# A new written-out order for a fused attention and expert kernel: SBUF work of two engines kept apart, four shared banks, seven fp32 dummies

## The chip, the cores and the metric

The kernel runs on one core of a Trainium2 chip. A core has five engines that run side by side and wait for each other through semaphores: TensorE (PE in the profile; its weight loads are PEld), VectorE (DVE), ScalarE (ACT), GpSimd (POOL) and SyncE (SP), which here only issues DMA transfers. Products of TensorE go to PSUM, eight banks of 128 x 512 fp32; everything else lives in SBUF. The metric is the device time of one execution in microseconds, the median of several.

## The reference

Inputs are `r`, `k`, `v`, `w` of shape 4 x 8 x 768 x 48 (batch, heads, time, head width), `u` of 8 x 48, and two weight matrices, 384 x 2048 and 2048 x 384. First a recurrent attention:

```python
for t in range(S):
    cur = einsum('bhd,bhe->bhde', u * k[t], v[t])
    y[t] = einsum('bhd,bhde->bhe', r[t], state + cur)
    state = w[t][..., None] * state + einsum('bhd,bhe->bhde', k[t], v[t])
```

Its output, as 3072 tokens of 384, goes through `h = x @ w_in`, `g = max(h, 0) ** 2`, and `out = g @ w_out`.

## The kernel before

**Tiling.** Time is cut into steps of 256 positions, three for each of the four batches: steps 0 to 11. Inside a step the recurrence is done by chunks of 128 in matrix form. Decays are multiplied up as sums of logarithms: `ww_` multiplies neighbouring w, `lw_` takes the logarithm, `cum_` sums it by a product with a triangle of ones into a PSUM tile `att`, `al_` forms a second exponent from the first, and `exp_` exponentiates. `rw_`, `kw_`, `ku_`, `qp_`, `vq_` are elementwise multiplies of SBUF tiles; `q_` is a sum over a row and `qs_`, `vs_`, `v_` are copies that cast or move rows. `rd_` multiplies r or k by the decays. The results are transposed, by TensorE (`tr_`, then the copy `rkt_`) in steps 0 to 3, and by DMA (`dtr_`) from step 4 on. Then `p_` multiplies keys by queries, `pm_` applies the mask, `su_`, `ts_` and `sn_` carry the state on, `y_` and `yc_` form the output, `ysb_` adds the term of the own position, and the result is transposed to `xT`, by TensorE (`yt_`, then `xt_`) in steps 0 to 5 and by DMA (`dyt_`) from step 6 on.

**The expert part.** For each step there are eight `m1_` (six products of 128 x 256 into one bank: two blocks of `x @ w_in`), eight `rl_` that evict such a bank with max(x, 0) into fp16, four `sq_` that square two of these groups, eight `m2_` (four products of 128 x 384, two output halves by four quarters of the sum), and two `os_` that evict the finished sum, each followed by a `store`. The weights come in eight fp32 blocks (`ld.n.i`, `ld.n.o`) and are cast to bf16 (`cast`). Block n of W_in serves `m1_` groups 2n and 2n + 1.

**PSUM.** Two `att` tiles take four banks. The other four are two named `bk` (numbers 0 and 1) and two named `m1_bank` (2 and 3). Before the change `m1_` (line 532) can use only the second pair and `m2_` (line 559) and its `os_` (line 566) only the first; transposes can go to any (`bf16_bank`), and a `p_` or a `su_` goes to an `att` tile, or split over a pair, where the letter `b` or `m` says so. A split `p_` is masked by two instructions (line 431) rather than one (line 434).

**Order.** `ORDER` (line 17) is a list of 864 words. Each names an operation, its step and part, the bank after a colon, and the engine after `=` where there is a choice (A ScalarE, V VectorE, G GpSimd). The operations are issued in this order, so each engine's own list, SP's list of loads, transposes and stores included, is the order of its words here; nothing reorders it on the chip. Where two engines depend on each other semaphores make them wait. `warm_.n.b` issues n dummy products of a cleared tile into bank b (4 and 5 are the `att` tiles); their results are never read.

What the prediction speaks of most is the part of `ORDER` up to the first `m1_`, the list of VectorE in it, and the spacing of `dtr_` to `p_`, `dyt_` to `m1_`, and `m1_` to `rl_`.

Of the kernel before, what the change touches and what calls it, by code (L numbers as in the profile page):

```python
# [22 lines left out]
tr_.1.0:1 ww_.2=G ld.2.i v_.1=A rkt_.1.0=V ysb_.0=V vs_.1.1=A warm_.4.2 p_.1.1:0 qp_.1=G su_.1:m ld.2.v
pm_.1.1 lw_.2 yt_.0:0 cum_.2:1 ld.3.i ts_.1.0=V rw_.2=G q_.1 exp_.2 kw_.2=G xt_.0=V vs_.1.0=A rd_.2.0 qs_.1=G
ac_.2 cast.i.1=A rd_.2.1 warm_.10.1 tr_.2.0:1 sn_.1.0 p_.1.0:0 ku_.2=G ts_.1.1=V yc_.1.1:1 tr_.2.1:0
cast.i.0=A pm_.1.0 ld.0.o m1_.0.3:0 ld.3.w rkt_.2.1=V m1_.0.2:1 vq_.1=G rkt_.2.0=V y_.1:1 rl_.0.3=A yc_.1.0:1
rl_.0.2=V p_.2.0:0 m1_.0.1:0 ld.1.o ysb_.1=V cast.i.2=G m1_.0.0:1 rl_.0.1=A pm_.2.0 yt_.1:0 ld.3.r rl_.0.0=A
m1_.0.5:0 v_.2=A xt_.1=V qp_.2=G sn_.1.1 m1_.0.4:1 rl_.0.5=A p_.2.1:1 su_.2:b sq_.0.0=A rl_.0.4=V ld.2.o
m1_.1.4:0 cast.i.3=G ts_.2.0=V pm_.2.1 m1_.1.5:1 rl_.1.4=A q_.2 sn_.2.0 m1_.1.3:0 rl_.1.5=A ld.3.o vs_.2.1=G
vs_.2.0=A yc_.2.0:0 yc_.2.1:0 rl_.1.3=V m1_.1.6:1 cast.o.0=G qs_.2=A m1_.1.0:0 ld.3.k rl_.1.6=V sq_.0.2=A  # L30
y_.2:0 rl_.1.0=V m1_.1.1:1 vq_.2=G m1_.1.7:0 rl_.1.1=V ld.3.v m2_.0.1.0:0 sq_.1.2=A rl_.1.7=V sq_.0.1=A
cast.o.1=G m1_.1.2:1 rl_.1.2=A ysb_.2=V m1_.0.7:0 ld.4.w ww_.3=G yt_.2:1 rl_.0.7=V m1_.0.6:1 xt_.2=V m2_.0.1.1
sq_.1.1=A rl_.0.6=V ld.5.w m1_.2.6:0 cast.o.2=G lw_.3 sq_.1.0=A rl_.2.6=A cum_.3:1 sq_.1.3=A rw_.3=G al_.3
ld.5.r m2_.0.0.0:1 m1_.2.7:1 m2_.0.0.1 cast.o.3=V exp_.3 sq_.0.3=A ld.4.k rd_.3.0 kw_.3=G m1_.2.1:0 rl_.2.7=A
ac_.3 m2_.0.1.2 m2_.0.0.2 rl_.2.1=V ku_.3=G m2_.0.0.3 rd_.3.1 ld.4.v m2_.0.1.3 vs_.3.0=A m1_.2.0:1 os_.0.1=V
qp_.3=G ld.5.v m1_.2.3:0 os_.0.0=V rl_.2.0=V tr_.3.1:0 rl_.2.3=A tr_.3.0:1 rkt_.3.1=V v_.3=A ld.4.r m1_.2.4:1
ww_.4=G rkt_.3.0=V m2_.1.0.0:0 rl_.2.4=A q_.3 ww_.5=G p_.3.1:0 vs_.3.1=A ld.6.k su_.3:1 pm_.3.1 p_.3.0:m
m2_.1.0.1 ts_.3.0=A lw_.4 sn_.3.0 ld.5.k pm_.3.0 m2_.1.0.2 qs_.3=A m2_.1.1.0:1 sq_.2.0=A vq_.3=G ts_.3.1=V
m2_.1.0.3 ld.6.w cum_.4:0 m2_.1.1.1 ku_.4=G ac_.4 al_.4 store.0.1 m1_.2.5:0 os_.1.0=A v_.5=A yc_.3.1:1 y_.3:1
lw_.5 kw_.4=G m1_.2.2:1 ld.6.r ysb_.3=V rl_.2.5=A m2_.1.1.2 exp_.4 sn_.3.1 rl_.2.2=V yt_.3:0 rw_.4=G cum_.5:1  # L40
xt_.3=V m2_.1.1.3 vs_.4.0=A ac_.5 sq_.2.1=A qp_.4=G al_.5 m1_.3.0:0 rd_.4.1 v_.4=A m1_.3.3:1 rd_.4.0 dtr_.4.1
m2_.2.0.0:0 rl_.3.0=A rw_.5=G rl_.3.3=A m2_.2.0.1 os_.1.1=V exp_.5 q_.4 dtr_.4.0 su_.4:0 sq_.2.2=A m1_.3.4:0
kw_.5=G rd_.5.0 ww_.6=G m2_.2.1.0:1 rl_.3.4=A ts_.4.0=V sq_.2.3=A m1_.3.5:1 vs_.4.1=A rd_.5.1 sn_.4.0
m2_.2.1.1 store.1.0 ts_.4.1=V rl_.3.5=V ku_.5=G m1_.3.6:0 store.1.1 m2_.2.1.2 qs_.4=A ld.7.w ld.6.v rw_.6=G
p_.4.1:1 rl_.3.6=A p_.4.0:0 pm_.4.1 pm_.4.0 m2_.2.1.3 lw_.6 vq_.4=G m1_.3.1:1 m1_.3.2:0 rl_.3.1=A su_.5:1
dtr_.5.1 dtr_.5.0 vs_.5.1=G sq_.3.0=A rl_.3.2=V yc_.4.0:0 yc_.4.1:0 sn_.4.1 y_.4:0 os_.2.1=V sq_.3.1=A
m1_.3.7:1 ysb_.4=V ld.7.v m2_.2.0.2 rl_.3.7=A ld.8.w kw_.6=G vs_.5.0=G yt_.4:1 ld.7.k sq_.3.3=A m2_.2.0.3
xt_.4=V cum_.6:0 al_.6 m1_.4.4:0 qp_.5=G os_.2.0=A ac_.6 m1_.4.7:1 ts_.5.0=V exp_.6 rl_.4.4=V m2_.3.0.0:1
rl_.4.7=A rd_.6.1 m1_.4.6:0 rd_.6.0 m2_.3.0.1 dtr_.6.1 m2_.3.1.0:0 ku_.6=G qp_.6=G sq_.3.2=A rl_.4.6=A q_.5
dtr_.6.0 p_.5.0:1 p_.5.1:0 vs_.6.0=A m1_.4.5:1 sn_.5.0 m2_.3.0.2 qs_.5=G rl_.4.5=A pm_.5.1 pm_.5.0 vq_.5=G  # L50
m1_.4.1:0 m1_.4.3:1 rl_.4.3=A store.2.1 ld.8.v m2_.3.0.3 rl_.4.1=V ld.8.k v_.6=A ww_.7=G y_.5:0 q_.6 os_.3.0=A
ld.7.r m1_.4.0:1 store.0.0 ld.9.k ww_.8=G yc_.5.0:0 qs_.6=A su_.6:1 yc_.5.1:0 ysb_.5=V vs_.6.1=A ts_.6.0=V
m1_.4.2:0 ld.8.r m2_.3.1.1 rl_.4.0=V yt_.5:1 xt_.5=V sn_.6.0 lw_.7 vq_.6=G rl_.4.2=A p_.6.0:0 m2_.3.1.2
sq_.4.3=A store.2.0 pm_.6.0 m1_.5.2:1 ku_.7=G m1_.5.6:0 ts_.6.1=V yc_.6.1:0 sq_.4.0=A rl_.5.2=A p_.6.1:1
rl_.5.6=A m2_.3.1.3 kw_.7=G pm_.6.1 sq_.4.2=A m1_.5.4:1 rw_.7=G m1_.5.3:0 os_.3.1=V rl_.5.4=A y_.6:0 sn_.6.1
rl_.5.3=A cum_.7:1 kw_.8=G ysb_.6=V al_.7 m2_.4.0.0:1 vs_.7.1=A m1_.5.7:1 m1_.5.5:0 v_.7=G dyt_.6 sq_.4.1=A
rl_.5.7=V qp_.7=G rl_.5.5=V m2_.4.1.0:0 exp_.7 ld.9.w ld.9.v m2_.4.0.1 ac_.7 rd_.7.0 sq_.5.1=A m2_.4.0.2
ku_.8=G rd_.7.1 sq_.5.3=A dtr_.7.0 m2_.4.0.3 m1_.5.0:1 lw_.8 m1_.5.1:0 rw_.8=G rl_.5.0=V su_.7:0 q_.7
rl_.5.1=A cum_.8:1 dtr_.7.1 m1_.6.3:1 qs_.7=A m1_.6.5:0 rl_.6.3=V ld.10.w qp_.8=G ac_.8 sq_.5.0=A m2_.4.1.1
os_.4.0=V ts_.7.0=V ld.11.w sn_.7.0 m1_.6.4:1 rl_.6.5=A al_.8 ww_.9=G m2_.4.1.2 ld.9.r rl_.6.4=V exp_.8  # L60
store.3.0 m2_.5.1.0:1 sq_.5.2=A rd_.8.1 ts_.7.1=V sn_.7.1 m1_.6.0:0 vs_.7.0=G vs_.9.1=A rd_.8.0 m2_.4.1.3
m2_.5.1.1 kw_.9=G rl_.6.0=A dtr_.8.0 p_.7.1:0 v_.8=A p_.7.0:1 vq_.7=G pm_.7.1 m1_.6.1:1 m2_.5.1.2 rl_.6.1=A
pm_.7.0 ku_.9=G m2_.5.1.3 sq_.6.0=A lw_.9 m1_.6.6:0 dtr_.8.1 store.3.1 q_.8 yc_.7.0:0 v_.9=A yc_.7.1:0
rl_.6.6=V rw_.9=G su_.8:1 y_.7:0 os_.5.1=A ts_.8.0=V m1_.6.2:1 ysb_.7=V os_.4.1=A cum_.9:1 m1_.6.7:0 al_.9
dyt_.7 m2_.5.0.0:1 rl_.6.2=V exp_.9 ww_.10=G rl_.6.7=V m2_.5.0.1 ac_.9 ld.10.r rd_.9.1 sq_.6.1=A sq_.6.2=A
sn_.8.0 qp_.9=G ld.10.k qs_.8=G store.4.1 m2_.5.0.2 ld.10.v rd_.9.0 m2_.5.0.3 m2_.6.1.0:0 vs_.8.1=G sq_.6.3=A
dtr_.9.0 vs_.8.0=A p_.8.0:m p_.8.1:0 pm_.8.0 su_.9:1 m2_.6.1.1 ts_.9.0=A pm_.8.1 m2_.6.1.2 lw_.10 m1_.7.4:0
# [564 lines left out]
```

## Time and profile before

| what | value |
|---|---|
| median of the runs | 182.77 us (lowest 182.61) |
| profiled execution, first to last instruction | 182.2 us |
| TensorE busy | 171.8 us |
| VectorE, ScalarE, GpSimd busy | 130.0, 132.7, 122.7 us |
| bytes moved by DMA | 35.8 MB |
| first `m1_` product | 26.99 us |
| end of the last `m2_` product | 178.84 us |

One of the three runs took 960.62 us; the median leaves it aside. The profiled execution's own time is its span, 182.2 us, and what lies outside the first and the last instruction; the median of the runs is 0.57 us longer than that span. Times in the profile count from the first instruction. A row of groups gives line, engine, operation, output and inputs, shapes and count, then busy microseconds, mean nanoseconds of one, and the idle time ahead of them with what ended it. A row of the timeline gives start and duration. In a row of the chain of waits stand start, duration, engine or queue, tile and line.

### The profile page before, as it was taken

Reading aid. Unit: us, or ns where it says so; the run is one execution under the profiler, and the core shown is the slowest. Engines: PE = TensorE matmul, PEld = TensorE weight load, DVE = VectorE, ACT = ScalarE, POOL = GpSimd, SP = SyncE. Lnnn points to the kernel's source line nnn. Section 1 sums busy time; section 2 is a strip of 40 time slices with the busy share of each in tenths; the row PEclk is TensorE's granted clock in tenths of the full one; section 3 lists DMA queues with packets and bytes.
Section 4 is the critical chain, followed back from the end, with each engine's and each line's share of the span. In section 5 each row is a group of like instructions: output and inputs, shape, how many; then the busy total and the mean of one; then the engine's idle time right before and its main releaser. Section 6 shows DMA issues by size and latency. Waiting matters only on the chain.

```text
span 182.2 us, 5695 instructions
## 1 busy us (share of the span) xinstructions
PE 171.8 (94%) x2385; PEld 123.4 (68%) x2385; DVE 130.0 (71%) x195; ACT 132.7 (73%) x235; POOL 122.7 (67%) x140
## 2 busy tenths in 40 slices
...
GB/s 138 263 263 240 221 359 350 337 314 311 234 274 230 261 158 270 99 247 130 239 296 205 193 270 172 252 189 193 171 109 195 150 47 0 86 144 33 0 86 130
DMA packets 79208, 35.81 MB, mean 197 GB/s; under 512 B 72400, under 2 KB 77648, under 8 KB 79184
## 3 DMA queue, kind: packets, MB, share of 16 engines
...
## 4 chain that ended last, share of the span: by engine, by line
PE 75%; SPq 10%; DMA 8%; ACT 4%; issue 1%; DVE 1%; ACTq 0%
PE bk L561 32%; PE m L536 32%; SPq L178 8%; DMA w_st<-in_moe_w_in_dram 5%; PE att L420 3%; DMA rT<-rdec_buf 2%; PE att L483 2%; PE att L493 2%; PE att L446 1%; ACT gt L545 1%; PE att L326 1%; ACT wi_sb L200 1%; PE bk L516 1%; SPq L188 1%; SPq L205 1%
## 5 line engine op out<-in xcount | busy, mean ns | idle before, releaser
L536 PE MATMUL m<-xT,wi_sb 128*128 128x256 bf16 x576 | 74.0, 273 | 1.3 <-ACT gt L545 1.2
L561 PE MATMUL bk<-wo_sb,gt 128*128 128x384 bf16 x384 | 71.9, 326 | 0.0
L536 PEld LDWEIGHTS <-wi_sb 128*128 128x128 bf16 x576 | 54.8, 98 | 13.0 <-issue 0.9
L561 PEld LDWEIGHTS <-gt 128*128 128x128 bf16 x384 | 36.9, 98 | 19.2
L545 ACT ACTIVATE gt<-m 128x512 f16<-128x512 f32 x56 | 33.0, 595 | 22.3 <-PE m L536 21.9
L553 ACT ACTIVATE gt<-gt 128x1024 bf16<-128x1024 f16 x42 | 43.3, 1051 | 1.4 <-DVE gt L547 1.1
L547 DVE TENSOR_SCALAR gt<-m 128x512 f16<-128x512 f32 x40 | 27.0, 686 | 9.6 <-PE m L536 9.3
L434 DVE TENSOR_TENSOR pmT<-att,mask 128x1024 bf16<-128x1024 f32 x20 | 23.9, 1218 | 4.5 <-PE att L420 4.5
L297 POOL TENSOR_TENSOR ku<-k_raw,u_bc 128x768 f32<-128x768 f32 x12 | 21.8, 1819 | 0.2 <-DMA u_bc<-in_u_dram 0.2
L302 POOL TENSOR_TENSOR ku<-ku,r_raw 128x768 f32<-128x768 f32 x11 | 20.7, 1881 | 0.2
L316 POOL TENSOR_TENSOR ku<-v_sh,qs 128x768 f32<-128x768 bf16 x11 | 16.3, 1479 | 4.9 <-ACT qs L277 4.8
L277 ACT CAST v_sh<-v_raw 64x384 bf16<-64x384 f32 x34 | 17.3, 508 | 0.4
L290 POOL TENSOR_TENSOR k_raw<-k_raw,w_raw 128x384 f32<-128x384 f32 x12 | 12.2, 1013 | 6.4 <-DMA k_raw<-in_k_dram 6.3
L286 POOL TENSOR_TENSOR r_raw<-r_raw,w_raw 128x384 f32<-128x384 f32 x12 | 12.0, 1000 | 6.4 <-DMA r_raw<-in_r_dram 6.4
L504 DVE TENSOR_TENSOR y_sb<-att,ku 128x768 bf16<-128x768 f32 x12 | 11.4, 953 | 5.5 <-issue 1.6
L461 POOL TENSOR_TENSOR S<-t_state,ac_buf 128x192 bf16<-128x192 f32 x20 | 10.2, 512 | 6.4 <-DVE t_state L456 3.4
L361 DVE TENSOR_TENSOR kdec_buf<-k_raw,att 128x768 bf16<-128x768 f32 x12 | 11.4, 949 | 3.4 <-ACT att L340 2.8
L358 DVE TENSOR_TENSOR rdec_buf<-r_raw,att 128x384 bf16<-128x384 f32 x24 | 12.1, 547 | 2.2 <-ACT att L340 1.1
L340 ACT ACTIVATE att<-att 128x768 f32<-128x768 f32 x12 | 9.6, 798 | 3.1 <-PE att L328 1.9
L568 ACT ACTIVATE o_sb<-bk 128x384 f32<-128x384 f32 x13 | 6.3, 485 | 7.4 <-PE bk L561 7.3
L307 DVE TENSOR_REDUCE q<-ku 128x16 f32<-128x768 f32 x12 | 11.3, 943 | 0.0
L578 PE MATMUL att<-warm 128*128 128x512 bf16 x27 | 9.1, 492 | 1.2 <-DVE half_ones L228 1.2
...
## 6 DMA issues: line engine op xcount, KB each, us to landing
...
rT<-rdec_buf SPq DMA_TRANSPOSE x16, 4.1
```

Of the source, the lines that this page charges most:

```text
L178: nc.sync.dma_start(out=t[:, hs, at:at + 2, :].rearrange("p h j d -> p h (j d)"), in_=src[b, hs, i * T:(i + 1) * T, :].rearrange("h (p j) ...
L277: copy(out[j * Q:(j + 1) * Q, c], src[c * Q:(c + 1) * Q, :, j])
L290: tensor_mul("kw_", s, h)(raw["k", s][:, hs, 0, :], raw["k", s][:, hs, 1, :], raw["w", s][:, hs, 1, :])
L297: tensor_mul("ku_", s, h)(tiles["ku", s][:, hs], raw["k", s][:, hs, 1:3, :], u_bc[:, hs, None, :].to_broadcast([C, n, 2, D]))
L302: tensor_mul("qp_", s, h)(ku, ku, raw["r", s][:, heads(h), 0:2, :])
L316: tensor_mul("vq_", s)(vq[:], tiles["vs", s][:], tiles["qs", s][:, :, :, None].to_broadcast([C, 2, H, D]))
L434: nc.vector.tensor_mul(pmT, ps_p[:].rearrange("p e (x t) -> p (e x) t", t=C), mk.to_broadcast([C, 8, C]))
L536: nc.tensor.matmul(ps1[:, j, :], wi_sb[:, n // 4, kk, n % 4 * 128:(n % 4 + 1) * 128], tiles["xT", s][:, :, kk, :], start=(kk == 0), stop=( ...
L545: nc.scalar.activation(rl, m1, AF.Relu, scale=RS)
L547: nc.vector.tensor_scalar(out=rl, in0=m1, scalar1=RS, scalar2=0.0, op0=ALU.mult, op1=ALU.max)
L553: nc.scalar.activation(gt, rl, AF.Square)
L561: nc.tensor.matmul(m2, gt[:, n, c * C:(c + 1) * C], wo_sb[:, n, :], start=(n == 0), stop=(n == NT - 1))
```

## The change

The whole of `ORDER` is replaced: same operations for the same steps, in another sequence, with other engines and other banks. Counted by words: on VectorE `ku_` 0 to 1, `kw_` 0 to 3, `rw_` 0 to 3, `qp_` 1 to 4, `vq_` 1 to 3, `ww_` 2 to 4, `vs_` 0 to 2, `sq_` 6 to 8, `cast` 1 to 2, `rl_` 40 to 35, `xt_` 6 to 3, with the reverse on GpSimd or ScalarE. Split `p_` go from four to seven. The words `warm_` go from eight, with 46 bf16 products, to three with seven products of fp32. Besides, `m1_`, `m2_` and `os_` take a bank number from 0 to 3, and an `m2_` sum begins with whichever quarter comes first in the list rather than with quarter 0.

```diff
 ORDER = """
-ld.0.w ld.0.k ld.0.r ld.0.u ld.1.w ww_.0=V lw_.0 warm_.11.5 cum_.0:0 kw_.0=G exp_.0 rd_.0.1 ld.0.v warm_.8.5
...
+ld.0.w ww_.0=V lw_.0 ld.0.r rw_.0=G warm_.3.4 cum_.0:0 exp_.0 rd_.0.0 ld.0.k kw_.0=G rd_.0.1 ld.1.w ww_.1=G
+ac_.0 lw_.1 warm_.2.5 tr_.0.0:0 tr_.0.1:2 cum_.1:0 rkt_.0.1=A ld.0.u rkt_.0.0=V ku_.0=V qp_.0=V ac_.1 q_.0
+exp_.1 p_.0.0:m ld.1.k ld.0.v ld.1.r p_.0.1:b pm_.0.1 qs_.0=A v_.0=A vs_.0.1=A kw_.1=G rd_.1.1 vs_.0.0=A
+rw_.1=V ku_.1=G qp_.1=G rd_.1.0 warm_.2.5 tr_.1.1:1 rkt_.1.1=A su_.0:1 ts_.0.0=V sn_.0.0 tr_.1.0:0 vq_.0=G
+rkt_.1.0=A pm_.0.0 y_.0:0 ts_.0.1=V ld.1.v v_.1=A sn_.0.1 ld.2.w yc_.0.1 p_.1.1:1 q_.1 pm_.1.1 vs_.1.1=A
+p_.1.0:b su_.1:m ww_.2=G ts_.1.0=V qs_.1=A ysb_.0=V pm_.1.0 yc_.1.0:1 ld.2.r sn_.1.0 ld.2.k yc_.1.1 lw_.2
+vs_.1.0=A ts_.1.1=V cum_.2:0 yt_.0:0 y_.1 kw_.2=V rw_.2=G exp_.2 rd_.2.0 rd_.2.1 vq_.1=G xt_.0=A tr_.2.0:1
+ld.1.i sn_.1.1 ld.0.i ac_.2 rkt_.2.0=A tr_.2.1:3 ysb_.1=V cast.i.1=G yt_.1:0 rkt_.2.1=V cast.i.0=A ld.2.i
+ku_.2=G yc_.2.0:1 p_.2.0:m xt_.1=V ld.2.v qp_.2=G p_.2.1:0 cast.i.2=G m1_.1.3:1 m1_.0.2:0 pm_.2.0 m1_.0.3:3
...
 """
@@
+    quad = bk + m1_bank
@@
-    warm = consts.tile([C, 512], BF16)
+    warm = consts.tile([C, 512], FP32)
@@ def m1_(s, g):
-        ps1 = tiles["m1", s, g] = m1_bank[int(slot["m1_", s, g])][:].rearrange("p (j t) -> p j t", j=2)
+        ps1 = tiles["m1", s, g] = quad[int(slot["m1_", s, g])][:].rearrange("p (j t) -> p j t", j=2)
@@
+    summed = {}
+
     def m2_(s, c, q):
         gt = tiles["gt", s]
-        m2 = bk[int(slot["m2_", s, c])][:, 0:DM]
-        for n in range(4 * q, 4 * q + 4):
-            nc.tensor.matmul(m2, gt[:, n, c * C:(c + 1) * C], wo_sb[:, n, :],
-                             start=(n == 0), stop=(n == NT - 1))
+        m2 = quad[int(slot["m2_", s, c])][:, 0:DM]
+        summed[s, c] = summed.get((s, c), 0) + 1
+        for n in range(4):
+            nc.tensor.matmul(m2, gt[:, 4 * q + n, c * C:(c + 1) * C], wo_sb[:, 4 * q + n, :],
+                             start=(summed[s, c] == 1 and n == 0), stop=(summed[s, c] == NT // 4 and n == 3))
@@ def os_(s, c):
-        m2 = bk[int(slot["m2_", s, c])]
+        m2 = quad[int(slot["m2_", s, c])]
@@ def warm_(n, i):
-            nc.tensor.matmul((bk + m1_bank)[i][:] if i < 4 else att[i - 4][:, 0, :], warm[:, 0:C], warm[:],
+            nc.tensor.matmul(quad[i][:] if i < 4 else att[i - 4][:, 0, :], warm[:, 0:C], warm[:],
                              start=True, stop=True)
```

The words around the transposes of step 9 read in the new list:

```
m1_.7.3:2 rl_.7.3=A sq_.6.2=A rw_.9=G lw_.10 ysb_.8=V m1_.7.2:3 rl_.7.2=V m1_.7.6:1 ld.9.v m1_.6.7:2 rl_.7.6=V
...
m1_.8.4:1 al_.10 ld.10.k os_.5.1=A m1_.8.3:3 m1_.8.2:2 vs_.9.1=G m1_.8.7:0 rl_.8.4=V dtr_.9.1 m1_.8.5:1 q_.9
dtr_.9.0 rl_.8.7=V sn_.9.0 sq_.7.2=A rl_.8.2=A rl_.8.3=A ac_.10 sq_.6.0=A m1_.7.1:2 m1_.8.1:0 m1_.8.0:3
ts_.9.1=V rl_.8.5=V rl_.7.1=A sq_.6.3=V ld.11.w rl_.8.1=A sq_.7.3=A m1_.8.6:2 vs_.9.0=A rl_.8.0=V p_.9.1:b
```

138 lines of the change are left out of this document (63 added, 75 removed).

## Prediction

> **What bounds the kernel now.** I read the page first, then the table of stretches, then the chain of waits, the timeline around the start, and the groups by form.
>
> ```profile
> PE 171.8 (94%) x2385; PEld 123.4 (68%) x2385; DVE 130.0 (71%) x195; ACT 132.7 (73%) x235; POOL 122.7 (67%) x140
> ```
>
> TensorE is busy 94% of the span; no other engine reaches 75%. The table of stretches (us, then busy PE, PEld, DVE, ACT, POOL with counts, granted clock, DMA share, GB/s) says where the missing 6% lies:
>
> ```profile
> 0.00:10.00 10.00, 8.81 (x39) 3.64 (x40) 4.78 (x12) 4.19 (x8) 6.01 (x17) 1.00 0.91 207
> 10.00:20.00 10.00, 7.40 (x141) 4.24 (x138) 8.89 (x12) 8.43 (x19) 7.25 (x8) 1.00 1.15 245
> 20.00:27.00 7.00, 5.63 (x119) 3.53 (x119) 6.64 (x11) 4.86 (x8) 6.61 (x10) 1.00 0.96 304
> 27.00:30.00 3.00, 2.34 (x63) 2.00 (x60) 3.00 (x5) 1.45 (x2) 1.27 (x1) 1.00 1.07 338
> 30.00:40.00 10.00, 9.40 (x153) 8.10 (x154) 7.40 (x11) 8.65 (x17) 9.16 (x9) 1.00 1.08 333
> ...
> 80.00:90.00 10.00, 9.45 (x190) 7.29 (x187) 7.24 (x10) 7.73 (x16) 8.77 (x13) 1.00 1.03 193
> ...
> 120.00:130.00 10.00, 9.92 (x109) 7.45 (x108) 7.01 (x10) 8.82 (x20) 9.73 (x10) 1.00 0.85 160
> ...
> 170.00:179.00 9.00, 8.83 (x59) 5.48 (x56) 1.56 (x3) 3.56 (x6) 0.00 (x0) 1.00 0.24 87
> ```
>
> From 27 us on TensorE is without work for only 0.66 + 0.60 + 0.55 + 0.08 + 0.17 = 2.1 us; every stretch left out here shows 10.00. So the run has three parts: a start of 27 us, a body of products without holes, a tail. The next rows, from the timeline (start, duration) and the chain, date them: the first dummies, the first exp, ten later dummies, the first W_in product (`m1_`), the cast of the W_in block that came last, and the end of the last products.
>
> ```profile
> 1.19 4.87 PE L578 MATMUL att<-warm 128*128 128x512 bf16 x11 [1.19 <-DVE half_ones L228]
> 6.84 0.80 ACT L340 ACTIVATE att<-att 128x768 f32<-128x768 f32 x1 [1.10 <-PE att L328]
> 22.11 2.32 PE L578 MATMUL bk<-warm 128*128 128x512 bf16 x10
> 26.99 1.47 PE L536 MATMUL m<-xT,wi_sb 128*128 128x256 bf16 x12
> 28.55 1.47 ACT L200 CAST wi_sb<-w_st 128x1536 bf16<-128x1536 f32 x1 [1.84 <-DMA w_st<-in_moe_w_in_dram]
> ...
> 171.68 7.16 PE bk L561 x44
> ```
>
> The body runs from 26.99 to 178.84: **151.85 us**. What follows (last eviction, store, landing) is 182.2 - 178.84 = **3.36 us**. The median of the runs, 182.77, stands 0.57 above this execution's span, which I add at the end.
>
> **The change, part by part.** The products themselves stay: 96 `m1_`, 96 `m2_`, and every product of the attention part occurs as often as before. An order cannot shorten a body without holes; it can only start it earlier, put more work ahead of it, or close holes. So the sum is: start of the body + 151.85 - work done ahead + change in holes + tail.
>
> *Work done ahead.* Ahead of the first `m1_` the new TensorE list has everything that the old one has there, and besides `y_.1`, `yc_.1.0`, `yc_.2.0`, `yt_.1`, `p_.2.0` and `p_.2.1`. The chain prices such pieces: two `yc_` (x32), a whole `y_`, a `yt_`, two `p_` (x32).
>
> ```profile
> 36.54 0.37 PE att L493 x32
> ...
> 72.03 0.51 PE att L483 x16
> ...
> 73.84 0.34 PE bk L516 x6
> ...
> 79.01 0.58 PE att L420 x32
> ```
>
> That is 0.37 + 0.51 + 0.34 + 0.58 = **1.80 us** off the body.
>
> *Start of the body.* The loads ahead of W_in blocks 1 and 0 are the same twelve inputs and `u`, in another order, so the blocks should land when they landed (cast of block 0 possible at 28.55, block 1 before that). Block 1, used first, is now cast by GpSimd, after `vq_.1` and `sn_.1.1`. But the first `m1_` of the new list is for step 1, and VectorE must by then have done both steps' share, `ysb_.1` and `xt_.1` last. Its list up to there, priced by groups (mean ns after the comma):
>
> ```profile
> L434 DVE TENSOR_TENSOR pmT<-att,mask 128x1024 bf16<-128x1024 f32 x20 | 23.9, 1218 | 4.5 <-PE att L420 4.5
> ...
> L358 DVE TENSOR_TENSOR rdec_buf<-r_raw,att 128x384 bf16<-128x384 f32 x24 | 12.1, 547 | 2.2 <-ACT att L340 1.1 <-ACT ac_buf L346 1.1
> ...
> L504 DVE TENSOR_TENSOR y_sb<-att,ku 128x768 bf16<-128x768 f32 x12 | 11.4, 953 | 5.5 <-issue 1.6 <-PE att L493 1.4 <-POOL ku L297 1.3
> ...
> L361 DVE TENSOR_TENSOR kdec_buf<-k_raw,att 128x768 bf16<-128x768 f32 x12 | 11.4, 949 | 3.4 <-ACT att L340 2.8 <-POOL S L461 0.4 <-POOL ku L302 0.3
> ...
> L307 DVE TENSOR_REDUCE q<-ku 128x16 f32<-128x768 f32 x12 | 11.3, 943 | 0.0
> ...
> L431 DVE TENSOR_TENSOR pmT<-m,mask 128x512 bf16<-128x512 f32 x8 | 5.1, 684 | 2.0 <-ACT v_sh L277 1.3 <-PE m L420 0.7
> ...
> L456 DVE TENSOR_TENSOR t_state<-S,att 128x192 f32<-128x192 bf16 x12 | 4.2, 346 | 1.4 <-POOL S L461 1.2 <-PE att L446 0.3
> ...
> L521 DVE COPY xT<-bk 128x768 bf16<-128x768 bf16 x6 | 3.3, 552 | 1.7 <-PE bk L516 1.6
> ...
> L389 DVE COPY rT<-bk 128x1024 bf16<-128x1024 bf16 x3 | 2.0, 679 | 0.0
> ...
> L302 DVE TENSOR_TENSOR ku<-ku,r_raw 128x768 f32<-128x768 f32 x1 | 0.9, 945 | 0.0
> ...
> L264 DVE TENSOR_TENSOR ww<-w_raw x2: 557/664/772, 4.6 to 10.2; 128x384 f32<-128x384 f32 x2
> ```
>
> Three `rd_` of r (two instructions, 1.09) 3.27; three of k 2.85; three split `pm_` (2 x 0.684) 4.11 and one whole 1.22; two `ysb_` 1.91; two `q_` 1.89; four `ts_` 1.38; two `rkt_` 1.36; `xt_.1` 0.55; and, new on VectorE, `ku_.0` and `qp_.0` at 0.945 and `rw_.1`, `kw_.2`. A multiply of that 128x384 shape lies between 0.557 (GpSimd at rest) and 0.772; I take 0.557, since the change keeps GpSimd quiet. Total **21.55 us**. It starts when `exp_.0` ends, 7.64 before.
>
> Ahead of that stand three fp32 dummies in place of eleven bf16 ones. No row shows an fp32 product; between the price of one bf16 dummy (4.87/11 = 0.44) and four of them (1.77), three last 1.3 to 5.3 us. I take the upper end, being four times the bf16 price for a type that is wider than bf16: 1.19 + 5.3, and a little for a tile of twice the bytes to clear, ends near 6.75 where the old ones ended at 6.06 (1.19 + 4.87). So `exp_.0` ends about 0.7 later, at 8.35; at the lower end it would not move. The Trainium skill, page "FP8 and Floating Point Precision", lists true FP32 as four passes through the array; by it the upper end holds, and no run here shows it yet. 8.35 + 21.55 = 29.9; with the start of a product the body begins at **30.0**, 3.0 later than now. Bounds: 28.0, if VectorE's work overlaps better and GpSimd's cast decides; 31.5, if VectorE is idle as much as between 10 and 27 us now (10 + 7 - 8.89 - 6.64 = 1.5). The later start costs more than the work ahead returns.
>
> *VectorE against GpSimd.* The second row below is the clash that the change removes: a GpSimd multiply of 1.815 took 2.546 beside VectorE's `vq_`, which took 1.683 where a 768-wide multiply takes 0.945.
>
> ```profile
> L302 POOL TENSOR_TENSOR ku<-ku,r_raw 128x768 f32<-128x768 f32 x11 | 20.7, 1881 | 0.2
> ...
> L302 POOL TENSOR_TENSOR ku<-ku,r_raw x11: 1807/1815/2546, 18.9 to 139.1; 128x768 f32<-128x768 f32 x11
> ...
> L316 DVE TENSOR_TENSOR ku<-v_sh,qs x1: 1683/1683/1683, 18.1 to 18.1; 128x768 f32<-128x768 bf16 x1
> ```
>
> The eleven take 20.7 us against 11 x 1.815 = 20.0, so all clashes on this line cost 0.7 us, and the engine is not the bound: worth nothing in the body. The Trainium skill, page "SBUF — State Buffer", section on the shared port pair, says that a VectorE instruction with two SBUF inputs and a GpSimd one that reads SBUF exclude each other for the whole instruction. The trace agrees in these two rows; by that rule the sixteen multiplies moved to VectorE would each cost GpSimd up to their length wherever the order fails to keep them apart.
>
> The price of the separation is where the work goes. Counted in the two lists, VectorE gains a `ku_`, three each of `kw_`, `rw_`, `qp_`, and two each of `ww_`, `vq_`, `vs_`, `sq_`, with a cast, and gives up five `rl_` and three `xt_`: about +10 us, to 140. GpSimd loses about 16, ScalarE 2. None overtakes TensorE on the whole run; in single stretches they may (below).
>
> *Four banks for all products.* A hole from a missing bank is rare now. All `m1_` products together, with what TensorE waited for ahead of them (last figures), and the two kinds of eviction:
>
> ```profile
> L536 PE MATMUL m<-xT,wi_sb 128*128 128x256 bf16 x576 | 74.0, 273 | 1.3 <-ACT gt L545 1.2
> ...
> L545 ACT ACTIVATE gt<-m 128x512 f16<-128x512 f32 x56 | 33.0, 595 | 22.3 <-PE m L536 21.9
> L547 DVE TENSOR_SCALAR gt<-m 128x512 f16<-128x512 f32 x40 | 27.0, 686 | 9.6 <-PE m L536 9.3
> ...
> 101.49 0.65 PE m L536 x6
> ```
>
> Only 1.3 of the 2.1 us stand ahead of an `m1_`, while the evictions waited 31 us for products. Sharing `bk` with `m1_` can return at most that 1.3. I give nothing, for the same banks now also hold `m2_` sums and split `p_`. The turned order inside an `m2_` sum and the start flag by first use cost nothing: same instructions. Seven fp32 dummies in place of 46 bf16 ones: none stood in the body, so leaving them out frees only time in which TensorE waited.
>
> *SP's list.* The DMA transposes are as many. Their landing, from issue:
>
> ```profile
> rT<-rdec_buf SPq DMA_TRANSPOSE x16, 4.1
> kT<-kdec_buf SPq DMA_TRANSPOSE x8, 4.6
> xT<-y_sb SPq DMA_TRANSPOSE x6, 2.8
> ```
>
> Between the last `dtr_` of a step and its first `p_` the old list has 4.3 us of products at least (step 4), the new one 2.6 in step 9 and 3.8 in step 6; between `dyt_` and its first `m1_` 3.3 at least before, and 2.3, 2.6 and 2.6 in steps 10, 8 and 11 now. Taken alone this opens holes of up to 2.0 + 0.8 + 0.5 + 0.2 + 0.2 = 3.7 us; where TensorE is behind its list they vanish. Against the old holes that could close (2.1) I take the change in holes as **zero**, with -2.1 and +3.7 as bounds. Tail: the last four products, an eviction on ScalarE and a store, as now: 3.36.
>
> **Sum.** 30.0 + 151.85 - 1.80 + 0 + 3.36 = 183.4; plus 0.57: **184.0 us**, 0.7% above now.
>
> **The rivals.** *Evictions fall behind (slower).* Place: the end of a run of 17 `m1_` (steps 6 to 8) that the new list has with only `cum_.10` and `su_.9` between, from `q_.9` to `sq_.8.1`. An `m1_` takes 0.65 us and one eviction of 0.60 (ScalarE) or 0.69 (VectorE), and a square for each pair besides. Summed over the lists, VectorE and ScalarE together have 8.8 us more work there than twice TensorE's, 4.4 each; the worst stretch of the old list has 5.4, 2.7 each, and no hole followed. Price: between 4.4 - 2.7 = 1.7 and 4.4, some 3: **187.0**. It decides once the four banks are full and TensorE waits for a `rl_`. For it: VectorE's ten microseconds more. Against: four banks let it run further ahead than two.
>
> *The start does not slip (faster).* If GpSimd's cast is the bound (28.0 at best) and half of the holes close: 28.0 + 151.85 - 1.80 - 1.05 + 3.36 + 0.57 = **180.9**. Against it: VectorE has no slack in the 21.55. Even with all holes closed at 28.0, 179.9 remains, so over 2% faster needs an earlier start as well.
>
> *TensorE goes slow for want of dummies.* Eleven dummies at 1.19 took 0.44 each, ten at 22.11 took 0.23, at a granted clock of 1.00 in both stretches: it starts slow, and is fast after some 5 us of work. The new list has no dummy after the second pair, and between 16 and 30 us, by the prices above, about half as much work as time. If it is slow again when the body begins, 4.87 us pass at half rate: +2.4, **186.4**. The Trainium skill, page "TensorE: Matmul & The Clock Gate", Part 1, describes half rate after an idle window of about 3.4 us; the trace agrees on the two rates, and shows no return to the slow one.
>
> **How the numbers follow.** Forecast 0.55, evictions 0.25, early start 0.13, slow TensorE 0.07. A difference under 2% (179.1 to 186.4) counts as none. Evictions pass 186.4 in three cases of four, slow TensorE in half, the forecast with a late start and all the late transposes rarely: slower 0.26. Faster 0.04: the early start's lower edge. The rest, 0.70, is within. Range 180.6 to 188.4: from just under the early start to the full 4.4 us of the evictions.
>
> **What would show it.** Right: the first `m1_` near 30 with VectorE full from 9 us on and `xT` its releaser; from there to the last product about 150 us. Early start: first `m1_` under 28.5. Evictions: `m1_` waiting for evictions (L545, L547) in the run of steps 7 and 8. Transposes: `p_.9` idle before it on a DMA. Slow TensorE: the first `m1_` lasting 1.3 us. fp32 dummies: 1.7 us each early. I am wrong altogether if a store held back or a load that comes late stops the body for several microseconds.

## The result, and the profile after

| | us |
|---|---|
| before, median of 4 | 182.78 |
| changed, median of 4 | 190.62 (188.31 to 194.08) |
| forecast | 184.0, range 180.6 to 188.4 |

The ratio to the kernel before is 1.0341, with a 95% interval of 1.0281 to 1.0402: slower by 3.4%. The median lies above the upper end of the range. Ratios here and below compare only executions close to the fastest of each kernel, 188.31 and 189.91 here, so that 1.0341 is less than 190.62 / 182.78. Run again beside later kernels, the changed kernel took 191.24 against 183.29 (1.0428, 1.0378 to 1.0477). The profiled execution is the longest of the four: 194.08, with a span of 192.3. One thing that differs from execution to execution is the outcome of a contest of two engines at 52 us, shown below; the trace of the repeated kernel (189.89, span 188.1) has the other outcome.

The page of the changed kernel: the line of busy times, TensorE's busy tenths in 40 slices of 4.8 us, and the granted clock in the same slices.

```profile
PE 175.6 (91%) x2353; PEld 126.2 (66%) x2353; DVE 146.9 (76%) x212; ACT 129.4 (67%) x228; POOL 112.1 (58%) x133
...
PE   6874789999938999999999999989989999999993
...
PEclk9999556999997999999999999999999999999999
```

TensorE was busy 171.8 us before and 175.6 now, with seven fp32 dummies in place of 46. VectorE was to gain 10 us and gained 17; GpSimd lost 11 and not 16. An instruction that is kept waiting counts as busy, so 5.4 of the 17 are the wait of one cast, shown below. TensorE's row has a hole in slice 12, and the clock has a stretch at half near the start and a dip behind the hole. The table of stretches (columns as in the prediction) dates them:

```profile
10.00:20.00 10.00, 6.17 (x128) 3.57 (x130) 9.93 (x15) 8.44 (x16) 7.22 (x5) 0.94 1.25 269
20.00:27.00 7.00, 5.16 (x142) 4.25 (x135) 6.70 (x11) 5.01 (x12) 6.32 (x8) 0.50 1.08 365
27.00:30.00 3.00, 3.00 (x67) 2.50 (x64) 2.52 (x5) 2.45 (x3) 2.92 (x3) 0.50 1.12 336
...
50.00:60.00 10.00, 6.06 (x82) 3.64 (x81) 9.97 (x6) 7.69 (x13) 9.14 (x9) 0.99 0.78 179
60.00:70.00 10.00, 10.00 (x85) 6.72 (x83) 8.20 (x14) 3.88 (x7) 0.00 (x0) 0.84 0.07 14
```

VectorE is full from 10 us on, as foretold. From 20 to 30 the granted clock is 0.50. Between 50 and 60 TensorE works 6.06 of 10 us while VectorE is busy for 9.97 with only six instructions. TensorE's timeline shows the fp32 dummies, the first W_in product, and the hole:

```profile
1.45 4.70 PE L582 MATMUL att<-warm 128*128 128x512 f32 x6 [1.45 <-DVE half_ones L229]
...
6.42 1.88 PE L582 MATMUL att<-warm 128*128 128x512 f32 x4
...
30.23 2.59 PE L537 MATMUL bk<-xT,wi_sb 128*128 128x256 bf16 x12
...
58.53 1.48 PE L565 MATMUL m<-wo_sb,gt 128*128 128x384 bf16 x8 [3.94 <-DVE wo_sb L201]
```

The body begins at 30.23, where the sum had 30.0. It lasts 158.7 us, to 189.0, where the sum had 151.85 - 1.80 = 150.0. Its first twelve products take 2.59 us; the first twelve took 1.47 before. At 58.53 a product has waited 3.94 us for VectorE's cast of W_out block 3. The two timelines beside it, VectorE first, then GpSimd:

```profile
50.93 1.21 DVE L435 TENSOR_TENSOR pmT<-att,mask 128x1024 bf16<-128x1024 f32 x1
52.06 6.42 DVE L201 CAST wo_sb<-w_st 128x1536 bf16<-128x1536 f32 x1
58.40 1.21 DVE L435 TENSOR_TENSOR pmT<-att,mask 128x1024 bf16<-128x1024 f32 x1
```

```profile
52.20 1.02 POOL L265 TENSOR_TENSOR ww<-w_raw 128x384 f32<-128x384 f32 x1
53.15 1.02 POOL L287 TENSOR_TENSOR r_raw<-r_raw,w_raw 128x384 f32<-128x384 f32 x1
54.11 1.83 POOL L298 TENSOR_TENSOR ku<-k_raw,u_bc 128x768 f32<-128x768 f32 x1
55.87 0.83 POOL L273 CAST v_bf<-v_raw 128x768 bf16<-128x768 f32 x1
56.65 1.01 POOL L291 TENSOR_TENSOR k_raw<-k_raw,w_raw 128x384 f32<-128x384 f32 x1
57.86 1.48 POOL L265 TENSOR_TENSOR ww<-w_raw 128x384 f32<-128x384 f32 x1 [0.20 <-ACT lw_buf L269]
```

In the kernel before, the same cast stood here:

```profile
45.31 1.03 DVE L200 CAST wo_sb<-w_st 128x1536 bf16<-128x1536 f32 x1
```

The cast that took 1.03 before takes 6.42. GpSimd works through five SBUF instructions, each beginning before the record of the last has ended, and the cast ends only behind the first gap, 57.66 to 57.86. Now GpSimd's `ww_`, 1.0 at rest, takes 1.48. The profiled execution's extra 10.1 us of span (192.3 - 182.2), and the 5.9 of the repeated kernel's, are taken apart further below.

### The profile page after: what moved, and what is told of

Its sections match the earlier page's. It is cut to its first block, busy times and chain, and to the rows that moved or that the text cites. A ratio compares the mean times of both kernels' runs of the same rounds, so it can differ in the third digit from the quotient of the medians.

```text
span 192.3 us, 5646 instructions
## 1 busy us (share of the span) xinstructions
PE 175.6 (91%) x2353; PEld 126.2 (66%) x2353; DVE 146.9 (76%) x212; ACT 129.4 (67%) x228; POOL 112.1 (58%) x133
## 4 chain that ended last, share of the span: by engine, by line
PE 71%; DVE 18%; DMA 3%; issue 3%; POOL 2%; ACT 1%; DVEq 0%
PE bk L565 17%; PE m L537 14%; PE m L565 13%; PE bk L537 13%; DVE wo_sb L201 3%; DMA xT<-y_sb 3%; PE att L421 2%; PE att L582 2%; PE att L484 2%; DVE kdec_buf L362 2%; DVE rdec_buf L359 2%; DVE pmT L432 2%; PE att L494 2%; DVE r_raw L287 1%; PE att L447 1%
## 5 line engine op out<-in xcount | busy, mean ns | idle before, releaser
L565 PE MATMUL bk<-wo_sb,gt 128*128 128x384 bf16 x208 | 40.2, 334 | 0.0
L537 PE MATMUL m<-xT,wi_sb 128*128 128x256 bf16 x306 | 39.8, 273 | 0.0
L537 PE MATMUL bk<-xT,wi_sb 128*128 128x256 bf16 x270 | 36.9, 279 | 0.6 <-DMA xT<-y_sb 0.6
L565 PE MATMUL m<-wo_sb,gt 128*128 128x384 bf16 x176 | 33.2, 327 | 4.0 <-DVE wo_sb L201 3.9
L546 ACT ACTIVATE gt<-m 128x512 f16<-128x512 f32 x38 | 22.2, 597 | 16.3 <-PE m L537 16.1
L548 DVE TENSOR_SCALAR gt<-bk 128x512 f16<-128x512 f32 x22 | 15.1, 686 | 6.6 <-PE bk L537 6.6
L546 ACT ACTIVATE gt<-bk 128x512 f16<-128x512 f32 x23 | 13.6, 596 | 6.5 <-PE bk L537 6.4
L303 POOL TENSOR_TENSOR ku<-ku,r_raw 128x768 f32<-128x768 f32 x8 | 14.5, 1817 | 0.5
L269 ACT ACTIVATE lw_buf<-ww 128x384 bf16<-128x384 f32 x12 | 6.2, 520 | 10.8 <-DVE ww L265 9.3
L548 DVE TENSOR_SCALAR gt<-m 128x512 f16<-128x512 f32 x13 | 8.8, 686 | 5.0 <-PE m L537 5.0
```

The lines of the kernel that those rows point to most:

```text
L303: tensor_mul("qp_", s, h)(ku, ku, raw["r", s][:, heads(h), 0:2, :])
L537: nc.tensor.matmul(ps1[:, j, :], wi_sb[:, n // 4, kk, n % 4 * 128:(n % 4 + 1) * 128], tiles["xT", s][:, :, kk, :], start=(kk == 0), stop=( ...
L546: nc.scalar.activation(rl, m1, AF.Relu, scale=RS)
L548: nc.vector.tensor_scalar(out=rl, in0=m1, scalar1=RS, scalar2=0.0, op0=ALU.mult, op1=ALU.max)
L565: nc.tensor.matmul(m2, gt[:, 4 * q + n, c * C:(c + 1) * C], wo_sb[:, 4 * q + n, :], start=(summed[s, c] == 1 and n == 0), stop=(summed[s, ...
```

## The experiments

The quoted expectations speak of three theories: A, TensorE's clock falls for want of dummies; B, VectorE's SBUF work is shut out by GpSimd; C, VectorE's longer list and its clashes everywhere. Ratios are to the kernel before on the same chip.

**Dummies.** The changed kernel with bf16 dummies, 46 of them, spread as far as the list allows:

```diff
-warm_.3.4 ... warm_.2.5 ... warm_.2.5          warm = consts.tile([C, 512], FP32)
+warm_.11.4 ... warm_.8.5 ... warm_.8.5         warm = consts.tile([C, 512], BF16)
+warm_.6.0 before tr_.1.0, warm_.2.4 before cum_.2, warm_.8.1 before tr_.2.0, warm_.3.3 before tr_.2.1
```

> The changed kernel with 46 bf16 dummies in place of the seven fp32 ones: eleven and eight where three and two stood, eight for the third pair, and six, two, eight and three more ahead of tr_.1.0, cum_.2, tr_.2.0 and tr_.2.1, where TensorE waited. Theory A (TensorE falls to half clock for want of work between 15 and 19 us, and the first m1_ run at half rate): no stretch under 1.00 before 50 us, first m1_ at 29 to 30, time 1.5 to 4 us below the changed kernel; the slow stretch after the wait at 54 to 58 us remains. Theory B (all is the VectorE cast of W_out block 3, shut out by GpSimd): clock as before or not, time unchanged within 1 us. Theory C (VectorE carries too much in the whole body): unchanged within 1.5 us.

Measured: 188.51 us (185.95 to 189.11), 1.0241 (1.0161 to 1.0321), where the changed kernel has 1.0341 and 1.0428 in its two sets: a gain of 1 to 2%, as theory A has it, with intervals that overlap in the first case. In the profiled execution the granted clock is full throughout, the first `m1_` stands at 29.61, and the cast took 1.00. That execution is the shortest; the other three took 188.5 to 189.1, and no trace shows why.

**The cast alone.** The block that was shut out goes to GpSimd:

```diff
-cast.o.3=V
+cast.o.3=G
```

> The changed kernel with one word changed: the cast of W_out block 3 on GpSimd in place of VectorE. Theory B: the cast takes 1.46 us instead of 6.42, TensorE's wait of 3.9 us at 54 us is gone or under 1 us, and with it the slow clock around 60 us; time 4 to 6 us below the changed kernel. Theory A alone: the first slow stretch stays, gain under 1.5 us. Theory C: VectorE's list is 6 us shorter but evictions stay late, gain under 2 us.

Measured: 194.06 us, 1.0581 (1.0535 to 1.0627): not a gain but a further loss. VectorE's timeline and TensorE's waits (total, times, longest) say why:

```profile
54.04 6.11 DVE L278 CAST v_sh<-v_raw 64x384 bf16<-64x384 f32 x2
```

```profile
PE att L484 <- DVE v_sh L278: 4.1, 1, 4.1
```

The wait passed to the next SBUF copy of VectorE, two small casts that take 0.7 together at rest. They end only behind GpSimd's chain of records that touch, which runs to 59.55. It is the place beside GpSimd's chain that is dear, not this cast.

**Both.** Dummies and cast together.

> Both edits of the two runs above. If A and B together are the cause: clock 0.99 or more over the span, time 181.5 to 184. If C holds as well: 185 or more, with TensorE waiting for VectorE in the middle of the body, from 120 to 150 us above all.

Measured: 192.75 us, 1.0525 (1.0485 to 1.0565), with the same wait of 4.1 us for `v_sh`. The expected gain failed for the same reason.

**The clock alone, in the kernel before.** Three words with the last sixteen of its 46 dummies go:

```diff
-warm_.2.2 ... warm_.4.2 ... warm_.10.1
```

> The kernel before without its last three groups of dummies (16 bf16 products after 15 us; 30 stay). Theory A: TensorE's clock falls to half between 18 and 27 us here too, the first m1_ run at half rate for 2 to 4 us, and the time is 184.3 to 187. If the slow clock comes from something else in the new order: clock and time as before, 182.8 within 0.6.

The granted clock in 40 slices of 4.55 us:

```profile
PEclk9999555999999999999999999999999999999999
```

Measured: 184.40 us against 183.19, 1.0057 (1.0019 to 1.0095). The half clock from 17 to 31 us is made at will by leaving dummies out, and costs 1.2 us by the medians, 1.0 by the ratio.

**The changed kernel again, and its dummies in bf16.** One kernel unchanged, one with 28 bf16 dummies (four for each fp32 one) at the same three places:

```diff
-warm_.3.4 ... warm_.2.5 ... warm_.2.5          warm = consts.tile([C, 512], FP32)
+warm_.12.4 ... warm_.8.5 ... warm_.8.5         warm = consts.tile([C, 512], BF16)
```

> The changed kernel once more, beside the runs below on one chip. All theories: 186 to 192, a cast of W_out block 3 or the vs_.3.1 behind it that lasts 4 to 6 us in most executions, and half clock between 19 and 32 us.

> The changed kernel with each fp32 dummy replaced by four bf16 ones at the same place (28). If the type of the dummies keeps TensorE from speeding up or staying fast, the half clock after 19 us goes and the time falls by 1 to 2 us. If only their number and place count: same clock rows and the same time as the changed kernel within 1 us; the first three last 5 us and the pair after cum_.0 about 2 us, as now.

Measured: 191.24 us, 1.0428 (1.0378 to 1.0477), and 189.72 us, 1.0349 (1.0328 to 1.0370); the medians are 1.5 us apart. The second kernel's executions lie within 189.5 to 190.3, the first's are spread from 189.89 to 193.93, so that not all of the 1.5 need be the type of the dummies. Both clocks fell to half near 19 us with dummies of either type at these three places; in bf16 the clock was full again at 29.6, ahead of the first `m1_`, with fp32 only at 32.4. The repeated kernel shows the contest at 52 us with another winner, first on VectorE, then on GpSimd:

```profile
52.12 0.99 DVE L201 CAST wo_sb<-w_st 128x1536 bf16<-128x1536 f32 x1
...
54.57 2.49 DVE L278 CAST v_sh<-v_raw 64x384 bf16<-64x384 f32 x2
```

```profile
52.25 1.73 POOL L265 TENSOR_TENSOR ww<-w_raw 128x384 f32<-128x384 f32 x1
53.93 1.00 POOL L287 TENSOR_TENSOR r_raw<-r_raw,w_raw 128x384 f32<-128x384 f32 x1
54.89 1.95 POOL L298 TENSOR_TENSOR ku<-k_raw,u_bc 128x768 f32<-128x768 f32 x1
56.78 0.96 POOL L273 CAST v_bf<-v_raw 128x768 bf16<-128x768 f32 x1
```

Here the cast came first, and GpSimd's multiply lasted 1.73 instead of 1.0. In both traces the cast's record begins 0.13 to 0.14 us ahead of the multiply's, so the records don't show what decides. The two small casts at 54.57 met GpSimd records that touch, like those of the first trace, and yet got in between them: the first ends at 55.15, just behind the record that ends at 54.93, the second at 57.06, behind the one that ends at 56.84. So a chain without a gap does not always keep VectorE out to its end.

**A hole for VectorE.** One word makes GpSimd wait, so that its chain has a gap where VectorE's copies stand:

```diff
-vq_.3=V
+vq_.3=G
```

> One word of the changed kernel: vq_.3 on GpSimd, where it stands ahead of ww_.4 in GpSimd's list and must wait for vs_.3.1 of VectorE. So GpSimd's list has a hole while VectorE does its cast and vs_.3.1, and both stay on VectorE. Theory B, in the form that GpSimd instructions following each other without a hole keep a VectorE copy out of SBUF until they end: the cast takes about 1.0 us and vs_.3.1 about 0.3 apiece, TensorE's wait of 4 us near 54 us is gone, the clock there stays at 1.00, time 184.5 to 187. If it is the length of VectorE's list and not the shut-out (Theory C): VectorE is only 1 us shorter, GpSimd 1.5 longer, and the time stays within 1.5 us of the changed kernel.

> The hole of the run before together with the 46 bf16 dummies: both suspected costs gone. If nothing else is lost, the forecast's own sum holds with the body starting near 29.6: 183 to 185, clock 1.00, holes in the body of about 2 us. Theory C: 186 or more.

The second kernel has the 46 dummies besides. GpSimd's row shows the hole:

```profile
54.12 1.47 POOL L317 TENSOR_TENSOR ku<-v_sh,qs 128x768 f32<-128x768 bf16 x1 [3.14 <-DVE v_sh L278]
```

Measured: 188.80 us, 1.0301 (1.0261 to 1.0340), and 188.34 us, 1.0280 (1.0235 to 1.0326). The cast takes 1.00 in both, and no wait of TensorE after 32 us exceeds 1.1. Against the changed kernel on the same chip the first gains 2.4 us, with the dummies 2.9. Not all of the 2.4 is the hole's: the two traces are 1.7 us apart, of which 1.1 lies in the products of the body, with a half clock that ends at 29.8 and not at 32.4, and only 0.2 in TensorE's gaps, the cast having won in both. Both kernels stay slower than foretold for theory B: it holds as a mechanism, but A and B together explain less than half of the 8 us. The clock of the second was not full either (0.973 to 1.0 on the mean of an execution), though at half only ahead of the body in the trace, from 12 to 16 and from 22 to 26 us. Its trace says what is left there, 3.7 us of span: the body begins 3.6 later (30.55 against 26.99), and TensorE is without work in it for no longer than before (1.8 against 1.9 us).

**The shut-out, in the kernel before.** The cast and its product move to where GpSimd is in a chain:

```diff
-m2_.0.0.1 cast.o.3=V exp_.3 ... ku_.3=G m2_.0.0.3 rd_.3.1
+m2_.0.0.1 exp_.3 ... ku_.3=G rd_.3.1 cast.o.3=V m2_.0.0.3
```

> The kernel before, with the VectorE cast of W_out block 3 and the product that needs it moved a few words later, so that the cast comes up (48 to 49 us) while GpSimd works through a chain of five SBUF multiplies whose only gap is 0.07 us (46.56 to 53.16 in the trace of before). Theory B (a VectorE SBUF copy is shut out until GpSimd's chain has a hole): the cast, 1.03 us before, lasts about 4 us, until 53.2, TensorE waits for it 3 to 4 us with the profile naming it, and the kernel is 2 to 4 us slower (1.2 to 2.2%). If the 0.07 us gap is already hole enough, the cast lasts 1.3 to 2 us and the loss is under 1 us. Rival (the cast was long in the changed kernel for another reason, such as its weights or its place): the cast lasts 1.0 us, and the time does not move.

VectorE, GpSimd, and TensorE's wait:

```profile
48.01 1.41 DVE L200 CAST wo_sb<-w_st 128x1536 bf16<-128x1536 f32 x1
```

```profile
46.77 1.82 POOL L297 TENSOR_TENSOR ku<-k_raw,u_bc 128x768 f32<-128x768 f32 x1
48.67 2.41 POOL L302 TENSOR_TENSOR ku<-ku,r_raw 128x768 f32<-128x768 f32 x1
```

```profile
PE bk L561 <- DVE wo_sb L200: 2.0, 1, 2.0
```

Measured: 185.20 us against 183.60, 1.0093 (1.0063 to 1.0122). The cast waits for the end of one GpSimd instruction (46.77 + 1.82 = 48.59), gets in through a gap of 0.08 us, and the next GpSimd multiply lasts 2.41 instead of 1.81. So a gap of 0.08 was hole enough here. The loss was larger than expected for that outcome: of TensorE's wait of 2.0 us the lengthening of the cast accounts for 0.4 (1.41 - 1.03), and the later place for the rest. So this run shows the clash and its small size here, and no shut-out of several microseconds.

**What is left: the multiplies given back.** From e7_hole_dummies, twelve multiplies after the start return to GpSimd, and two `vs_`, two `sq_` to ScalarE; or three multiplies ahead of the start; or both:

```diff
-ww_.5/8/11=V kw_.4/11=V rw_.6/10=V qp_.4/7/9=V vq_.7/11=V vs_.3.1=V vs_.7.0=V sq_.2.3=V sq_.4.1=V
+ww_.5/8/11=G kw_.4/11=G rw_.6/10=G qp_.4/7/9=G vq_.7/11=G vs_.3.1=A vs_.7.0=A sq_.2.3=A sq_.4.1=A
```

```diff
-rw_.1=V kw_.2=V ku_.0=V
+rw_.1=G kw_.2=G ku_.0=G
```

> The changed kernel with its 46 bf16 dummies and vq of step 3 on GpSimd (as e7_hole_dummies), and besides all of VectorE's twelve SBUF multiplies after the start (ww of 5, 8, 11; kw of 4, 11; rw of 6, 10; qp of 4, 7, 9; vq of 7, 11) back on GpSimd, two vs and two sq back on ScalarE. Theory C (what is left of the loss, besides the later start, is VectorE's list made longer by these operations and by clashes of the two engines): 1.5 to 3 us less than e7_hole_dummies, 185.5 to 187, with no SBUF operation of VectorE over 1.5 us after 32 us. Rival (the residue lies in the start and in the new list of TensorE itself): within 0.7 us of 188.3. Third way: GpSimd, for which the order was not planned, comes late and the kernel is slower than 189.

> As e7_hole_dummies, with rw of 1, kw of 2 and ku of 0 given back from VectorE to GpSimd. Step 'start of the body' (VectorE's full list decides when the first W_in product can begin): the list is shorter by 0.95 + 2 x 0.56 = 2.1 us of work, and the first m1_ comes 1 to 2.5 us earlier than 30.55, at 28 to 29.5, and the time falls by as much. Rival (GpSimd's chain, the loads or the cast of W_in block 1 decide the start): first m1_ at 30 or later, no gain.

> Both together: the twelve multiplies after the start and the three ahead of it on GpSimd again, with 46 bf16 dummies. If start and VectorE's list each carry their share: 183.5 to 186, the sum of both gains. If the new sequence of TensorE itself costs the rest: 186.5 or more.

Measured: 189.96 us, 1.0356 (1.0295 to 1.0417); 187.62 us, 1.0204 (1.0130 to 1.0278); 190.45 us, 1.0380 (1.0326 to 1.0434). The first went the third way: GpSimd and ScalarE are now late, and TensorE waits 1.9 us for a `v_sh` of ScalarE. The second has its first `m1_` at 30.77, not earlier:

```profile
PE bk L375 <- DVE kdec_buf L362: 2.7, 1, 2.7
```

With three multiplies less, VectorE's list is no longer what decides; it waits for GpSimd instead, which is shown by VectorE's own timeline:

```profile
11.88 1.76 DVE L303 TENSOR_TENSOR ku<-ku,r_raw 128x768 f32<-128x768 f32 x1 [1.65 <-POOL ku L298]
```

So GpSimd is just behind VectorE at the start. These three kernels could not tell where the rest lies, because they disturb an order made for the other division.

**The two halves exchanged.** Start of one list, body of the other. e12: the order of before up to `xt_.1`, then the changed order with `vq_.3=G`. e13: the changed order with 46 dummies up to its first `m1_`, then the order of before.

```diff
 e12: ld.0.w ld.0.k ld.0.r ... yt_.1 ... xt_.1=V (before) | sn_.1.1 yc_.2.0 qp_.2=G p_.2.1 m1_.1.3 ... (changed)
 e13: ld.0.w ww_.0=V lw_.0 ... p_.2.1 cast.i.2=G (changed) | ld.3.i ld.0.o m1_.0.3 ld.3.w m1_.0.2 ... (before)
```

> The order of before up to xt of step 1 (first W_in product at 27 us there), then the changed order for all that is left, with vq of step 3 on GpSimd as in e7_hole_dummies. If the later start is what remains of the loss (3 to 3.5 us of e7's 5): 184.6 to 185.6 us. If the body of the new list carries it (VectorE's longer list, its clashes with GpSimd, the finer cut of TensorE's products): 187 or more, with holes of TensorE after 30 us or a body longer than 151.85 us by 2 us or more.

> The changed order up to its first W_in product, with the 46 bf16 dummies of e1_dummies, then the order of before for all that is left. The prediction's own sum, start 3.0 to 3.5 us later and 1.8 us of work done ahead, gives 1.2 to 1.7 us above before: 184.5 to 185.5, if the body of before stays without holes. If the start alone carries the whole rest of the loss: 187.5 or more.

Their first W_in products:

```profile
26.67 1.47 PE L541 MATMUL m<-xT,wi_sb 128*128 128x256 bf16 x12
```

```profile
29.79 1.48 PE L541 MATMUL bk<-xT,wi_sb 128*128 128x256 bf16 x12
```

Measured: 187.13 us, 1.0206 (1.0165 to 1.0246) with the old start, and 186.03 us, 1.0151 (1.0112 to 1.0190) with the new one. The body of the new list costs 3.7 us though it begins as early as before, and the new start costs 2.6, where the sum gave 1.2 to 1.7; a hole of 1.4 at the seam (bank of `pm_.2.0`) is made by the joining.

**The multiplies alone, in the kernel before.** The same twelve words, nothing else:

```diff
-ww_.5/8/11=G kw_.4/11=G rw_.6/10=G qp_.4/7/9=G vq_.7/11=G
+ww_.5/8/11=V kw_.4/11=V rw_.6/10=V qp_.4/7/9=V vq_.7/11=V
```

> The kernel before with the twelve SBUF multiplies that the change moves to VectorE after the start (ww of 5, 8, 11; kw of 4, 11; rw of 6, 10; qp of 4, 7, 9; vq of 7, 11) moved there, and nothing else. The prediction's step (VectorE gains 8 us of work, off the path, a clash lengthens an engine that is not the bound): within 0.8 us of 183.4. If the clashes themselves reach TensorE: VectorE's multiplies last over 1.1 us on the mean, TensorE gets new waits for VectorE's tiles, and the kernel is 2 us slower or more. If GpSimd, with some 16 us less to do, was late here and there: faster by up to 1 us.

Groups on VectorE, then TensorE's timeline:

```profile
L302 DVE TENSOR_TENSOR ku<-ku,r_raw 128x768 f32<-128x768 f32 x4 | 4.6, 1143 | 0.0
...
L316 DVE TENSOR_TENSOR ku<-v_sh,qs 128x768 f32<-128x768 bf16 x3 | 3.6, 1193 | 0.8 <-POOL v_sh L277 0.8
...
L286 DVE TENSOR_TENSOR r_raw<-r_raw,w_raw 128x384 f32<-128x384 f32 x2 | 2.7, 1356 | 0.0
L290 DVE TENSOR_TENSOR k_raw<-k_raw,w_raw 128x384 f32<-128x384 f32 x2 | 2.3, 1174 | 0.0
```

```profile
64.51 0.44 PE L446 MATMUL att<-v_bf,kdec_buf 64*64 64x48 bf16 x32 [0.46 <-DVE rdec_buf L358]
...
110.27 0.43 PE L446 MATMUL att<-v_bf,kdec_buf 64*64 64x48 bf16 x16 [0.47 <-DVE pmT L434]
117.20 0.44 PE L446 MATMUL att<-v_bf,kdec_buf 64*64 64x48 bf16 x32 [0.31 <-DVE rdec_buf L358]
122.03 0.81 PE L536 MATMUL m<-xT,wi_sb 128*128 128x256 bf16 x6 [0.80 <-DVE gt L547]
```

Measured: 187.12 us against 183.06, 1.0211 (1.0176 to 1.0246). This part alone costs **4.1 us** in the order of before. Two of the four groups hold a multiply that VectorE had before, too (0.94 in the first, 1.68 in the second). One by one, the twelve take 12.5 us where 8.6 were priced at rest, 1.04 on the mean: seven are near their price, one of 0.95 took 1.09, and four are far longer (1.80, 1.51 and 1.20 for 0.56, and 1.58 for 0.95). TensorE waits for VectorE at four places where the kernel before has no such wait between 40 and 150 us. How much is the lengthening and how much the mere addition to VectorE's list is not separated.

## Why the prediction was wrong, step by step

*Start of the body:* the number was right, 30.0 forecast, 30.23 found, 29.5 to 30.9 in all kernels with the new start; the way there was partly luck. The fp32 dummies cost near the upper end, 4.70/3 = 1.57 us each while slow and 1.88/2 = 0.94 when fast; yet `cum_.0` was not late for them, since they end at 6.15, and `exp_.0` ended at 7.42 and not at 8.35. VectorE's list then took 22.3 us, to the end of `xt_.1` at 29.75, where 21.55 were priced, and one of its rows is a clash of the kind that the change was to remove, `rw_.1` beside GpSimd's `qp_.1`, at 1.99 where I took 0.557:

```profile
14.86 1.99 DVE L287 TENSOR_TENSOR r_raw<-r_raw,w_raw 128x384 f32<-128x384 f32 x1
```

The last 0.5 us passed in TensorE's own products ahead of the first `m1_`, at half clock, so that `xT` was not its releaser. And e10 shows GpSimd just behind VectorE.

*Work done ahead:* nearly right. Summing start to start over all rows of TensorE's timeline, without the gaps, the body of before takes 149.94 and the rest of the same list behind the new start (e13) 148.62: 1.3 us returned, 1.8 forecast.

*"An order cannot shorten a body without holes", and so its products were held at a fixed length:* wrong. Two kernels at full clock with the same products ahead of the body, by the same sum: 148.62 with the old order (e13), 150.28 with the new (e1). The finer cut of the new list, with small products more often alone among large ones, costs **1.7 us**; the other pair, before and e12, gives 2.3. An example from e1, TensorE's timeline:

```profile
143.75 0.31 PE L494 MATMUL att<-S,rT 64*64 64x48 bf16 x16
144.00 0.82 PE L565 MATMUL m<-wo_sb,gt 128*128 128x384 bf16 x4
144.75 0.31 PE L494 MATMUL att<-S,rT 64*64 64x48 bf16 x16
144.99 0.82 PE L565 MATMUL m<-wo_sb,gt 128*128 128x384 bf16 x4
```

Each `yc_` by itself holds TensorE 0.25 us from start to start, 0.50 for the two; side by side they took 0.37 in the prediction's row. Besides, a large product that stands ahead of a group of 64 x 64 ones holds TensorE 0.09 us longer than one ahead of another large one: the first four `m2_` products above take 0.75, where four ahead of an `m1_` take 0.65. There are 24 such places in e1 and 19 in e13, and the small products, which stand in 42 stretches instead of 35, take 1.2 us more in all: together the 1.7. One rival is that the sum counts part of a wait as a product: in e14, where TensorE's list is untouched, it rises by 1.6 (151.54 against 149.94), in eleven products that are 0.07 to 0.19 us longer, most of them ahead of a wait. Among the large products e1 has no more of these than e13, four against five; for the small ones it is not separated.

*VectorE against GpSimd, "worth nothing in the body":* this is **the step that failed** and that the experiments single out, beside the fixed length above and the dummies below. I priced it by one line of the kernel before, where GpSimd loses 0.7 us and is not the bound, and read the moved instructions as a matter of load (sixteen multiplies, I wrote; the two lists give fourteen multiplies and two `vs_`). I charged GpSimd alone, where VectorE, which feeds TensorE, waits as well, and I left out the casts. The runs show a wait of 3.9 to 4.1 us of TensorE for a VectorE cast in three traces (the changed kernel, e2, e3), a gain of 2.4 us by the median when one word opens a hole for it (e6, part of it the clock's), and 4.1 us for twelve multiplies moved in the order of before (e14). The Trainium skill, page "SBUF — State Buffer", section "Who interferes with whom", has a VectorE instruction with two SBUF inputs contend with a GpSimd one that reads SBUF, and a cast in a two-port mode with GpSimd, one of the two being held off for a whole instruction. The rows agree (1.73 against 1.0, 2.41 against 1.81), but the cast of 6.42 was held off through five instructions. The 4.1 us of e14 is no term of the changed kernel, though: with the same twelve multiplies on VectorE, in the order made for them, TensorE's gaps in the body come to 1.0 us in e1 and 1.2 in e10, less than the 1.9 of before.

*Dummies, "frees only time in which TensorE waited", and the slow rival at 0.07:* this step failed too, and the rival came true. Its mechanism was right and its size at the start of the body too large: 2.4 us was forecast, 1.1 us is seen in the first twelve products (2.59 - 1.47), 1.2 in e4. In the profiled execution a second stretch at half clock follows the hole at 54 us (0.84 on the mean from 60 to 70); e2 and e3, with holes of 4.1 us, have one that begins within 1.3 us of the hole's end as well.

*Four banks, late transposes, evictions:* right that they are worth little. In the changed kernel's trace TensorE never waited over 0.6 us for a DMA transpose, and the run of steps 7 and 8 has no hole ahead of an eviction.

Taken together, by the same sums, in us of span:

| | profiled execution | repeated kernel (e0) |
|---|---|---|
| later start | 3.2 | 3.5 |
| work ahead | -1.3 | -1.3 |
| finer cut | 1.7 | 1.7 |
| lower clock (body without gaps 153.10 and 151.62, against 150.28 in e1) | 2.8 | 1.3 |
| gaps (5.67 and 2.73, against 1.91) | 3.8 | 0.8 |
| tail | -0.1 | -0.1 |
| sum | 10.1 | 5.9 |

The row of the clock takes all that the body has over e1 for the clock, so it is an upper bound. My sum had the first two rows, and that is why it came to +1.2. It put the next three at nothing. Which of them weighs most differs from execution to execution: the gaps where the cast loses the contest, the cut and the clock where it wins. The medians can't be taken apart in this way, since one execution of each kernel has a trace.
